# Second layer of a fused kernel: blocks 0 and 1 turned by another engine, rows' parts moved ahead of weight splits

## The chip, the cores and the metric

The kernel runs on one core of one Trainium2 chip. The metric is the device time of one execution in microseconds (us). Five engines work side by side, each with a queue of its own: TensorE (PE in the profile; PEld is its weight load), VectorE (DVE), ScalarE (ACT), GpSimd (POOL) and SyncE (SP), which here only issues DMAs.

## The reference, cut to what matters

Three layers are chained: causal attention with a decay, a mixture of experts that sends each of 2304 tokens to one of 8 experts, and a dense layer on all tokens.

```python
x = attn(q, k, v, f)                          # 2304 tokens x 512
e_idx = np.argmax(x @ w_gate + modality_bias[modality_id], axis=1)
for e in range(8):                            # first layer: 512 -> 1024 -> 512
    mask = e_idx == e
    h = np.maximum(x[mask] @ w1[e], 0.0)
    out[mask] = gate_w[mask, None] * (h @ w2[e])
h = out @ w_in                                # second layer: 512 -> 2048 -> 512
g = np.maximum(0.01 * h, h)
return (g @ w_out).astype(np.float32)
```

## The kernel before, in words

Every product of float32 operands is made from two parts: a high part (a rounded copy, made by ScalarE) and a low part (the difference, made by VectorE), so that each product costs three matmuls: high by high, high by low, low by high. Names end in h and l for the parts: xh, xl (an expert tile's turned rows), w1h, w1l and w2h, w2l (an expert's weights), hh, hl (the turned activations of an expert tile), fxh, fxl (the second layer's turned rows), gh, gl (its activations).

**First layer.** Tokens are sorted by expert into tiles of 128. There are at least 18 of them (NSTAT), and at most 25 (NS); the number is known at run time, and in this run it is 20, tiles 0 to 19. `step(t)` (L1165) does, for tile t, its first product (`gemm1`, 24 matmuls, into h), and for tile t-1 the turning of its activations (`trh`, L1114: 8 transposes into two PSUM tiles th, then hh by ScalarE and hl by VectorE) and its second product (`gemm2`, L1124: two halves of 12 matmuls into yp). Between these two halves `trx` (L207) turns the rows of tile t+1: 4 transposes into tx, then xh, xl. yp is a single PSUM bank. `yout` (L1129) empties it: ScalarE writes ys (a pool of two buffers, tag "ys"), GpSimd copies an index column into it and scatters the rows to yd in DRAM. For tiles from 17 on, `yout` comes at the beginning of a later step: `step(19)` begins with `yout(17)`. `split(t, 0, k)` and `split(t, 1, k)` make the parts of the first and the second weights where the expert changes, under a condition that ScalarE and VectorE read, and have SyncE load the next weights.

Inside a step all five engines keep the program's order, as it is written (`ordered(tc, MS2)`, all engines named). Steps 18 and later sit in nested conditions, and the last one leads to `tail` (L1142): here `tail(19)`, with `yout(18)`, `trh(19)`, both halves of `gemm2` for tile 19 and `yout(19)`.

**Second layer.** The rows in yd are taken in four blocks of 512 and one of 256. `xload(b)` (L994) fetches a block into xr, which has one buffer. Blocks 0 and 1 come as rows, four DMAs of 128 rows each; 16 transposes by TensorE turn a block (`xts`, L1013), and ScalarE and VectorE make fxh and fxl. Blocks 2 to 4 come in pieces of 128 elements such that VectorE alone can turn them (STREAM_TRANSPOSE, into a buffer xq), after which fxh and fxl are made from xq. Block 0 is turned in `tail`: three groups of four transposes ahead of the first half of `gemm2`, one between the halves. Block 1 is turned in the second layer's visits 2 and 3, one group of four transposes ahead of `g1` and one behind it in each. Their PSUM pool pfx has a single buffer.

`visit(v)` (L1407) does `g1` (12 matmuls into u, then us, gh, gl by ScalarE and VectorE in turn) for one piece of the hidden layer, and `g2` (12 matmuls into a) for the piece of the visit before. In visits 0 to 4 only TensorE's order is written out; a scheduler at build time orders the other engines by when it expects things to be ready, except that `keep_in_program_order` puts an instruction behind the one written before it on its engine.

Of the kernel before, what the change touches and what calls it, by code (L numbers as in the profile page):

```python
# [9 lines left out]
F32 = mybir.dt.float32  # L10
F32R = mybir.dt.float32r
BF16 = mybir.dt.bfloat16
I32 = mybir.dt.int32
# [6 lines left out]
P = 128  # L20
B, H, S, D = 4, 8, 576, 64
BH = B * H
DM = H * D
# [6 lines left out]
XW = DM + 1  # L30
NSTAT = NTOK // P
# [4 lines left out]
NKB, NFB, NGB = DM // P, FF // P, DFF // P  # L36
FT = 512
GS = 4
NFIX = NTOK % FT
FIX = NTOK - NFIX  # L40
# [4 lines left out]
SIDE = 2  # L45
SP = 2.0
TE = 3
TX = 3
PST = 3
MS = ['PE', 'Activation', 'DVE', 'Pool', 'SP']  # L50
MS2 = ['PE', 'Activation', 'DVE', 'Pool', 'SP']
# [25 lines left out]
def fused(ctx: ExitStack, tc, qk0, qk2, vp, f, mid, wg, mb, w1, w2, w_in, w_out, out):  # L77
    nc = tc.nc
# [7 lines left out]
    yd = dr.tile([NTOK, XW], F32, name="yd")  # L86
# [120 lines left out]
    def trx(t, pool, tag):  # L207
        ps = pool.tile([P, 512], F32, tag=tag, name=f"tx{t}")
        for k in range(NKB):
            nc.tensor.transpose(ps[:, k * P:(k + 1) * P], xg[t % 2][:, k * P:(k + 1) * P], ident)  # L210
        nc.scalar.copy(xh[t % 2], ps)
        nc.vector.tensor_sub(xl[t % 2], ps, xh[t % 2].bitcast(F32))
# [769 lines left out]
    t0 = 0  # L982
# [11 lines left out]
    def xload(b):  # L994
        t0, n = blocks[b]
        r = xp.tile([P, FT // P, XW], F32, tag="xr", name=f"xr{b}")
        if b > 1:
            XR[b] = r.rearrange("p c d -> p (c d)")[:, :4 * n]
            for j in range(4):
                nc.sync.dma_start(XR[b][32 * j:32 * j + 32].rearrange("b (q c) -> b q c", c=P), yd[t0:t0 + n, j * P:(j + 1) * P].rearrange("(q b) c -> b q c", b=32))  # L1000
            if t0 < FIX:
                nc.sync.dma_start(tid[:, t0 // P:(t0 + n) // P].unsqueeze(2), yd[t0:t0 + n, DM:].bitcast(I32).rearrange("(c p) o -> p c o", p=P))
            return
        for i in range(n // P):
            XR[b, i] = r[:, i]
            nc.sync.dma_start(XR[b, i], yd[t0 + i * P:t0 + (i + 1) * P, :])

    X = {}

# [3 lines left out]
    def xts(b, sb, psums, part=None):  # L1013
        t0, n = blocks[b]
        if b not in X:
            xtile(b, sb)
        xh, xl = X[b]
        for i in range(n // P) if part is None else part:
            c = slice(i * P, (i + 1) * P)
            if b > 1:  # L1020
                t = XQ[0].tile([P, 512], F32, tag="xq", name=f"xq{b}_{i}")
                tc.keep_in_program_order(nc.vector.transpose(t.rearrange("p (i k c) -> p i k c", i=4, k=NKB), XR[b][:, i * 512:(i + 1) * 512].rearrange("p (i c k) -> p i k c", i=4, k=NKB)))
                t = t.rearrange("p (i k c) -> p k i c", i=4, c=32)
                h, l = (x[:, :, c].rearrange("p k (i c) -> p k i c", c=32) for x in (xh, xl))
                tc.keep_in_program_order(nc.scalar.copy(h, t))
                tc.keep_in_program_order(nc.vector.tensor_sub(l, t, h.bitcast(F32)))
                continue
            r = XR[b, i]
            nc.gpsimd.tensor_copy(tid[:, t0 // P + i:t0 // P + i + 1], r[:, DM:].bitcast(I32))
            rk = r[:, :DM].rearrange("p (c k) -> p k c", k=NKB)  # L1030
            pool, tag = psums[i % len(psums)]
            ps = pool.tile([P, 512], F32, tag=tag, name=f"fx{b}_{i}")
            for k in range(NKB):
                nc.tensor.transpose(ps[:, k * P:(k + 1) * P], rk[:, k], ident)
            yield
            ps = ps.rearrange("p (k c) -> p k c", c=P)
            nc.scalar.copy(xh[:, :, c], ps)
            nc.vector.tensor_sub(xl[:, :, c], ps, xh[:, :, c].bitcast(F32))
            yield

    def xtr(*a):
        for _ in xts(*a):
            pass
# [47 lines left out]
    with tc.tile_pool(name="rt2", reuse_waits="tile", bufs=1) as rt2, \  # L1091
# [10 lines left out]
        w2l = [mw.tile([P, 2, DM], F32R, name=f"w2l{k}") for k in range(4)]  # L1102
        WL["2h"], WL["2l"] = w2h, w2l
        ysc = []
        hh = mw.tile([P, FF], F32R, name="hh")
        hl = mw.tile([P, FF], F32R, name="hl")
        gc = mw.tile([P, 2], F32, name="gc")
# [13 lines left out]
                nc.scalar.copy(hh[:, c], ps)  # L1121
                nc.vector.tensor_sub(hl[:, c], ps, hh[:, c].bitcast(F32))  # L1122

        def gemm2(t, k0, k1):  # L1124
            for k in range(k0, k1):
                for i, (ap, wp) in enumerate(((hh, w2h), (hh, w2l), (hl, w2h))):
                    nc.tensor.matmul(yp, lhsT=ap[:, k * P:(k + 1) * P], rhs=wp[k // 2][:, k % 2, :], start=(k == 0 and i == 0), stop=(k == NFB - 1 and i == 2))  # L1127

        def yout(t):  # L1129
            m, i = at_slot(oidx, t)  # L1130
# [11 lines left out]
        def tail(t):  # L1142
            with ordered(tc, MS4):
                if t >= LATE:
                    yout(t - 1)
                trh(t)
                ps = [(pmx, "tx"), (pma, "h"), (pmb, "h"), (pm0, "th")]
                xs_ = [xts(0, xp0, [p], [i]) for i, p in enumerate(ps)]
                for x in xs_[:3]:
                    next(x)  # L1150
                next(xs_[0])
                if t >= NSTAT:
                    split(t, 1, 3, True)
                gemm2(t, 0, 4)
                next(xs_[3])
                for x in xs_[1:]:
                    next(x)
                gemm2(t, 4, NFB)
                yout(t)

# [4 lines left out]
        def step(t):  # L1165
            nx = t + 1 < NS
            if t > LATE:
                yout(t - 2)
            if not t:
                with tc.issue_after(st["late"].ins):  # L1170
                    split(t, 1, 0)
                    split(t, 1, 1)
            if t == K1 - 1:
                flags(1, N2)
            keepg(t)
            if t > LATE:
                split(t, 0, 3)
            if t + 2 < NS and t + 2 != K1:
                gather(t + 2)
            if t:  # L1180
                gemm1(t, 0, 2, (pma, pmb)[t % 2], "h")
            aside(t, "load")
            if 0 < t < TE:
                trh(t - 1)
            if nx:
                split(t + 1, 0, 0)
            aside(t, "a1")
            aside(t, "a2")
            if t >= TE:
                trh(t - 1)  # L1190
            if t > NSTAT:
                split(t - 1, 1, 2)
            aside(t, "b")
            if nx:
                split(t + 1, 0, 1)
            aside(t, "pool")
            if t:
                gemm1(t, 2, 3, (pma, pmb)[t % 2], "h")
            if nx and t < NSTAT:
                split(t + 1, 0, 2)  # L1200
            if t:
                gemm1(t, 3, 4, (pma, pmb)[t % 2], "h")
                keep(t)
            if t > NSTAT:
                split(t - 1, 1, 3)
            if nx and t >= NSTAT:
                split(t + 1, 0, 2)
            if nx and 0 < t < LATE:
                split(t + 1, 0, 3)
            if t:  # L1210
                gemm2(t - 1, 0, 4)
            if nx and (0 < t < TX or t >= NSTAT - 1):
                trx(t + 1, pmx, "tx")
            if t:
                split(t, 1, 0)
                split(t, 1, 1)
            if nx and TX <= t < NSTAT - 1:
                trx(t + 1, pmx, "tx")
            if t == K1:
                next(fini, 0)  # L1220
            aside(t, "d")
            if t:
                gemm2(t - 1, 4, 8)
            if t < NSTAT:
                split(t, 1, 2)
            if 0 < t < LATE:
                yout(t - 1)
            if t < NSTAT:
                split(t, 1, 3)

        def finish():
            cnt, full, used = runb, early["full"], early["used"]
# [101 lines left out]
    with tc.tile_pool(name="fx", reuse_waits="tile", bufs=1) as fx, \  # L1334
# [5 lines left out]
         tc.tile_pool(name="pfu", reuse_waits="tile", bufs=3, space=PSUM) as pfu:  # L1340
        for i in range(GS, NSET):
            wset(fx, i)
        XQ.append(xq)
        G = {}
        A = {}
        Y = {}
# [60 lines left out]
        def visit(v):  # L1407
            b, fb = seq[v]
            parts = {}
            if fb < GS and b + 1 < NBK:  # L1410
                for k, i in (((2, 0), (2, 1), (3, 2), (3, 3)) if b == 0 else ((1, 0), (2, 1), (2, 2), (3, 3))):
                    if k == fb and i < blocks[b + 1][1] // P:
                        parts[i] = lambda b=b, i=i: xtr(b + 1, fx, [(pfx, "x")], [i])
            for i in sorted(parts)[:1 if v < GS else 2]:
                parts.pop(i)()
            g1(b, fb)
            for i in sorted(parts):
                parts.pop(i)()
            if v in XV:
                xload(XV[v])  # L1420
            if v:
                b, fb = seq[v - 1]
                g2(b, fb)
                if b == NBK - 1 and fb + NSET < NGB:
                    for i in range(2):
                        for _ in wpart(fb + NSET, i):
                            pass
                if v in WV:
                    for _ in wpart(*divmod(2 * GS + WV.index(v), 2)):
                        pass  # L1430
# [53 lines left out]
```

## Time and profile before

| | before |
|---|---|
| median of 3 runs | 857.75 us (857.01 to 859.49) |
| profiled execution, its own time | 857.52 us |
| span of that execution | 855.8 us |
| outside the span | 1.72 us |
| TensorE busy | 847.4 us, 99% of the span |
| TensorE's share of the chain that ended last | 94% |
| VectorE, ScalarE, GpSimd busy | 56%, 47%, 16% |
| granted TensorE clock | 1.0 of full speed in all 40 slices |

The span is the time from the first to the last instruction that the profiler saw. A busy TensorE is a queue of overlapping matmuls: a matmul of 128x512 is shown as 0.39 us long, and the next one starts 0.23 us after it. So the start of one instruction to the start of the next tells what it costs, and a larger distance is a stall even where no idle time is shown. The chain that ended last adds such distances up.

### The profile page before, as it was taken

Reading aid. Unit: us, or ns where it says so; the run is one execution under the profiler, and the core shown is the slowest. Engines: PE = TensorE matmul, PEld = TensorE weight load, DVE = VectorE, ACT = ScalarE, POOL = GpSimd, SP = SyncE. Lnnn points to the kernel's source line nnn. Section 1 sums busy time; section 2 is a strip of 40 time slices with the busy share of each in tenths; the row PEclk is TensorE's granted clock in tenths of the full one; section 3 lists DMA queues with packets and bytes.
Section 4 is the critical chain, followed back from the end, with each engine's and each line's share of the span. In section 5 each row is a group of like instructions: output and inputs, shape, how many; then the busy total and the mean of one; then the engine's idle time right before and its main releaser. Section 6 shows DMA issues by size and latency. Waiting matters only on the chain.

```text
span 855.8 us, 14440 instructions
## 1 busy us (share of the span) xinstructions
PE 847.4 (99%) x4724; PEld 700.8 (82%) x4724; DVE 479.0 (56%) x890; ACT 403.4 (47%) x857; POOL 133.2 (16%) x311
## 2 busy tenths in 40 slices
PE   8999999999999999999999999999999999999998
PEld 5888888888887888888888888888888888888887
DVE  7678777778757335233214456686338933473334
ACT  6888878877266355333323344553224422242222
POOL 5102222351146122112121000000000000001111
PEclk9999999999999999999999999999999999999999
DMA  6776787976385254132322231132002300011112
GB/s 210 194 188 178 204 214 201 235 206 207 94 295 190 64 173 137 59 96 75 100 53 66 51 74 50 54 119 75 0 1 74 102 22 1 1 50 50 49 50 74
DMA packets 36579, 92.72 MB, mean 108 GB/s; under 512 B 7017, under 2 KB 12809, under 8 KB 36490
## 3 DMA queue, kind: packets, MB, share of 16 engines
q1 hardware_dynamic: 31834, 76.95, 31.4%
q0 software_dynamic: 4640, 14.71, 5.5%
q8 instruction: 40, 0.66, 0.3%
q14 instruction: 49, 0.40, 0.1%
q10 hardware_dynamic: 16, 0.00, 0.0%
HBM read 131.63 MB, written 14.99 MB: 171 GB/s over the span
## 4 chain that ended last, share of the span: by engine, by line
PE 94%; DMA 2%; ACT 2%; DVE 1%; issue 0%; POOL 0%; SPq 0%; DVEq 0%
PE u L1358 23%; PE a L1378 23%; PE h L222 13%; PE yp L1127 13%; PE pv L547 5%; PE pt L535 3%; PE sc L446 2%; PE th L1119 2%; PE sc L447 2%; DMA aq<-aq 1%; PE xo L571 1%; PE tx L210 1%; ACT p L461 1%; PE pt L525 1%; PE sc L498 1%; PE sc L500 1%
## 5 line engine op out<-in xcount | busy, mean ns | idle before, releaser
L1360 ACT COPY us<-u 128x512 f32<-128x512 f32 (+1 forms) x80 | 43.4, 543 | 169.9 <-PE u L1358 169.5
L1361 DVE SCALAR_TENSOR_TENSOR us<-u,us 128x512 f32<-128x512 f32 (+1 forms) x80 | 50.9, 637 | 125.6 <-ACT us L1360 124.2
L1358 PE MATMUL u<-fxh,wloi 128*128 128x512 f32 (+1 forms) x320 | 117.2, 368 | 0.0
L1358 PE MATMUL u<-fxl,whii 128*128 128x512 f32 (+1 forms) x320 | 117.2, 368 | 0.0
L1358 PE MATMUL u<-fxh,whii 128*128 128x512 f32 (+1 forms) x320 | 116.3, 368 | 0.0
L1378 PE MATMUL a<-whio,gh 128*128 128x512 f32 x280 | 109.3, 391 | 0.0
L1378 PE MATMUL a<-wloo,gh 128*128 128x512 f32 x280 | 109.1, 390 | 0.0
L1378 PE MATMUL a<-whio,gl 128*128 128x512 f32 x280 | 101.9, 389 | 0.0
L461 ACT ACTIVATE p<-sc,nm 128x128 f32<-128x128 f32 (+3 forms) x128 | 66.1, 525 | 24.6 <-DVE nm L456 20.1
L1391 POOL DMA_INDIRECT out<-acc,tid x16 | 16.0, 1001 | 363.9 <-DVE acc L1385 343.7
L1358 PEld LDWEIGHTS u<-fxh,wloi 128*128 128x128 f32 x320 | 60.3, 188 | 10.5
L1358 PEld LDWEIGHTS u<-fxl,whii 128*128 128x128 f32 x320 | 60.3, 188 | 10.3
L1358 PEld LDWEIGHTS u<-fxh,whii 128*128 128x128 f32 x320 | 60.2, 188 | 10.3
L1363 ACT CAST gh<-us 128x512 fp32r<-128x512 f32 (+1 forms) x76 | 44.5, 586 | 49.1 <-DVE us L1361 39.0
L1364 DVE TENSOR_TENSOR gl<-us,gh 128x512 fp32r<-128x512 f32 (+1 forms) x76 | 49.2, 647 | 31.4 <-ACT gh L1363 29.9
L1122 DVE TENSOR_TENSOR hl<-th,hh 128x512 fp32r<-128x512 f32 x40 | 25.8, 686 | 71.9 <-ACT hh L1121 71.9
L456 DVE TENSOR_REDUCE nm<-sc 128x2 f32<-128x256 f32 (+1 forms) x64 | 51.1, 820 | 24.7 <-PE sc L452 18.7
L1127 PE MATMUL yp<-w2h,hh 128*128 128x512 f32 x160 | 64.5, 403 | 0.0
L1127 PE MATMUL yp<-w2h,hl 128*128 128x512 f32 x160 | 62.9, 393 | 0.0
L1127 PE MATMUL yp<-w2l,hh 128*128 128x512 f32 x160 | 62.5, 391 | 0.0
L1378 PEld LDWEIGHTS a<-whio,gl 128*128 128x128 f32 x280 | 52.5, 188 | 11.0
L1378 PEld LDWEIGHTS a<-whio,gh 128*128 128x128 f32 x280 | 52.6, 188 | 10.8 <-ACT gh L1363 0.4
(344 smaller groups left out, 1675.8 us busy)
## 6 DMA issues: line engine op xcount, KB each, us to landing
w1r<-w SPq DMA_DIRECT2D x86, 512.0 KB
w2r<-w SPq DMA_DIRECT2D x82, 512.0 KB
rwi<-w_in SPq DMA_DIRECT2D x16, 512.0 KB
rwo<-w_out SPq DMA_DIRECT2D x16, 512.0 KB
raw<-qk SPq DMA_DIRECT2D x14, 576.0 KB
vt<-vp SPq DMA_DIRECT2D x16, 320.0 KB
bk<-aq SPq DMA_DIRECT2D x14, 288.0 KB
bq<-raw SPq DMA_DIRECT2D x14, 288.0 KB
```

Of the source, the lines that this page charges most:

```text
L222: nc.tensor.matmul(Hp[t][:, n, :], lhsT=xp[t % 2][:, k * P:(k + 1) * P], rhs=wp[k][:, n * 512:(n + 1) * 512], start=(k == 0 and i == 0), s ...
L456: nc.vector.tensor_reduce(nm, view, axis=AX.X, op=ALU.max, negate=True)
L461: st["exp"] = nc.scalar.activation(pt[:, j, :], view[:, j, :], AF.Exp, bias=nm[:, j:j + 1], scale=1.0, accum_out=sms[g % 3][:, c, j:j + 1])
L547: nc.tensor.matmul(pv_[64 * j:64 * j + 64, q0:w], lhsT=vt[:, j, b, :], rhs=sb[:, j, b, q0:w], start=(b == 0), stop=(b == blocks[-1][0]))
L1122: nc.vector.tensor_sub(hl[:, c], ps, hh[:, c].bitcast(F32))
L1127: nc.tensor.matmul(yp, lhsT=ap[:, k * P:(k + 1) * P], rhs=wp[k // 2][:, k % 2, :], start=(k == 0 and i == 0), stop=(k == NFB - 1 and i == 2))
L1358: nc.tensor.matmul(ps, lhsT=w[:, k * P:(k + 1) * P], rhs=x[:, k, :], start=(i == 0), stop=(i == 3 * NKB - 1))
L1360: nc.scalar.copy(us, ps)
L1361: nc.vector.scalar_tensor_tensor(us, ps, 0.01, us, ALU.mult, ALU.max)
L1363: nc.scalar.copy(gh, us)
L1364: nc.vector.tensor_sub(gl, us, gh.bitcast(F32))
L1378: nc.tensor.matmul(A[b][i], lhsT=x[:, c], rhs=w, start=(first and m == 0), stop=(last and m == 2))
```

## The change

- `TX` goes. `trx(t + 1)` stands ahead of `split(t, 1, 0)` and `split(t, 1, 1)` in every step from 1 on; before, it stood behind them in steps 3 to 16.
- Block 0 is fetched in pieces, as blocks 2 to 4 are, with its token numbers by a DMA of its own instead of four copies on GpSimd. VectorE turns it. Its parts 0 and 1 stand in `step(18)` behind `trx(19)`, parts 2 and 3 at the end of `step(18)`. The 16 transposes in `tail` go. The buffers that VectorE turns into come from the "ys" pool.
- `gemm2`'s first half in `tail` puts its four low-part matmuls (hl) last.
- Block 1 is fetched half in pieces, half as rows. All four of its parts stand in visit 3 ahead of `g1`: parts 0 and 1 turned by VectorE, parts 2 and 3 by four transposes of TensorE each.

```diff
-TX = 3
@@ xload(b)
+        m = n // 2 if b == 1 else n
+        XR[b] = r.rearrange("p c d -> p (c d)")[:, :4 * m]
+        for j in range(4):
+            nc.sync.dma_start(XR[b][32 * j:32 * j + 32].rearrange("b (q c) -> b q c", c=P), yd[t0:t0 + m, j * P:(j + 1) * P].rearrange("(q b) c -> b q c", b=32))
+        for i in range(m // P, n // P):
             XR[b, i] = r[:, i]
             nc.sync.dma_start(XR[b, i], yd[t0 + i * P:t0 + (i + 1) * P, :])
+        if t0 < FIX:
+            nc.sync.dma_start(tid[:, t0 // P:(t0 + m) // P].unsqueeze(2), yd[t0:t0 + m, DM:].bitcast(I32).rearrange("(c p) o -> p c o", p=P))
@@ xts(b, sb, psums, part)
-            if b > 1:
-                t = XQ[0].tile([P, 512], F32, tag="xq", name=f"xq{b}_{i}")
-                tc.keep_in_program_order(nc.vector.transpose(...))
+            if (b, i) not in XR:
+                t = XQ[-1](b, i)
+                pin = tc.keep_in_program_order if b else (lambda x: x)
+                pin(nc.vector.transpose(...))
...
+                pin(nc.scalar.copy(h, t))
+                pin(nc.vector.tensor_sub(l, t, h.bitcast(F32)))
@@ first layer
+        XQ.append(lambda b, i: m2.tile([P, XW], F32, tag="ys", name=f"xq{b}_{i}")[:, :512])
@@ gemm2(t, k0, k1, late=False)
+            terms = [(k, i) for k in range(k0, k1) for i in range(3)]
+            if late:
+                terms = [x for x in terms if x[1] < 2] + [x for x in terms if x[1] == 2]
@@ tail(t)
-                ps = [(pmx, "tx"), (pma, "h"), (pmb, "h"), (pm0, "th")]
-                xs_ = [xts(0, xp0, [p], [i]) for i, p in enumerate(ps)]
-                for x in xs_[:3]:
-                    next(x)
-                next(xs_[0])
                 if t >= NSTAT:
                     split(t, 1, 3, True)
-                gemm2(t, 0, 4)
-                next(xs_[3])
-                for x in xs_[1:]:
-                    next(x)
+                gemm2(t, 0, 4, True)
+                if t < NSTAT:
+                    for i in range(4):
+                        xtr(0, xp0, None, [i])
                 gemm2(t, 4, NFB)
@@ step(t)
-            if nx and (0 < t < TX or t >= NSTAT - 1):
+            if nx and t:
                 trx(t + 1, pmx, "tx")
+            if t == NSTAT:
+                for i in range(2):
+                    xtr(0, xp0, None, [i])
             if t:
                 split(t, 1, 0)
                 split(t, 1, 1)
-            if nx and TX <= t < NSTAT - 1:
-                trx(t + 1, pmx, "tx")
...
             if t < NSTAT:
                 split(t, 1, 3)
+            if t == NSTAT:
+                for i in range(2, 4):
+                    xtr(0, xp0, None, [i])
@@ visit(v)
-                for k, i in (((2, 0), (2, 1), (3, 2), (3, 3)) if b == 0 else ((1, 0), (2, 1), (2, 2), (3, 3))):
+                for k, i in (((3, 0), (3, 1), (3, 2), (3, 3)) if b == 0 else ((1, 0), (2, 1), (2, 2), (3, 3))):
...
-            for i in sorted(parts)[:1 if v < GS else 2]:
+            for i in sorted(parts):
                 parts.pop(i)()
             g1(b, fb)
```

## Rows read from the trace of the kernel before

**Rows 1.** The page, part 1: busy us of each engine, share of span, instructions

```profile
PE 847.4 (99%) x4724; PEld 700.8 (82%) x4724; DVE 479.0 (56%) x890; ACT 403.4 (47%) x857; POOL 133.2 (16%) x311
```

**Rows 2.** Chain that ended last, steps 4 and 5: start us, us, engine tile line xcount

```profile
260.76 1.18 DVE w2l L177
261.95 0.61 DVE xl L212
262.60 2.13 PE h L222 x8
...
265.61 2.78 PE h L222 x12
```

**Rows 3.** Timeline of ScalarE, step 4: start us, us, instruction, count [idle before <-releaser]

```profile
257.63 2.00 ACT L173 CAST w2h<-w2r 128x1024 fp32r<-128x1024 f32 x2
```

**Rows 4.** Timeline of VectorE, step 4

```profile
257.24 2.42 DVE L177 TENSOR_TENSOR w1l<-w1r,w1h 128x1024 fp32r<-128x1024 f32 x2
```

**Rows 5.** Timeline of VectorE, step 18

```profile
433.22 0.69 DVE L212 TENSOR_TENSOR xl<-tx,xh 128x512 fp32r<-128x512 f32 x1 [5.10 <-ACTq L189]
```

**Rows 6.** Timeline of VectorE, second layer, block 2's parts 1 and 2

```profile
488.59 1.07 DVE L1022 STREAM_TRANSPOSE xq<-xr 128x512 f32<-128x512 f32 x1
490.35 0.69 DVE L1026 TENSOR_TENSOR fxl<-xq,fxh 128x512 fp32r<-128x512 f32 x1 [0.69 <-ACT fxh L1025]
490.96 1.08 DVE L1022 STREAM_TRANSPOSE xq<-xr 128x512 f32<-128x512 f32 x1
```

**Rows 7.** Timeline of ScalarE, step 19 and the tail

```profile
435.43 0.69 ACT L1133 ACTIVATE ys<-yp,gc 128x512 f32<-128x512 f32 x1 [2.24 <-PE yp L1127]
436.15 0.19 ACT L1112 COPY gc<-xg 128x1 f32<-128x1 f32 x1
449.06 1.06 ACT L1121 CAST hh<-th 128x512 fp32r<-128x512 f32 x2
```

**Rows 8.** Timeline of TensorE: step 19's second product, tail's first low-part matmul

```profile
441.62 0.39 PE L1127 MATMUL yp<-w2h,hh 128*128 128x512 f32 x1
441.85 0.39 PE L1127 MATMUL yp<-w2l,hh 128*128 128x512 f32 x1
444.38 0.60 PE L210 MATMUL tx<-ident,xg 128*128 128x128 f32 x4
450.49 0.50 PE L1127 MATMUL yp<-w2h,hl 128*128 128x512 f32 x1
```

**Rows 9.** Timeline of GpSimd: scatter of tile 16, block 1's last token numbers

```profile
428.78 1.03 POOL L1135 DMA_INDIRECT yd<-ys,oidx  x1 [14.05 <-DMA w1r<-w]
467.10 0.19 POOL L1029 COPY tid<-xr 128x1 int32<-128x1 int32 x1 [2.07 <-DMA xr<-yd]
```

**Rows 10.** Chain that ended last, the tail

```profile
448.61 1.45 PE fx L1034 x12
450.06 3.00 PE yp L1127 x12
453.06 0.47 PE fx L1034 x4
453.53 2.76 PE yp L1127 x12
```

**Rows 11.** Timelines of TensorE, ScalarE, VectorE, visit 2: one group of block 1's transposes

```profile
464.36 0.63 PE L1034 MATMUL fx<-ident,xr 128*128 128x128 f32 x4
464.75 0.48 PE L1358 MATMUL u<-fxh,whii 128*128 128x512 f32 x1
465.09 0.59 ACT L1037 CAST fxh<-fx 128x512 fp32r<-128x512 f32 x1 [1.31 <-PE fx L1034]
465.71 0.69 DVE L1038 TENSOR_TENSOR fxl<-fx,fxh 128x512 fp32r<-128x512 f32 x1 [1.21 <-ACT fxh L1037]
469.86 0.69 DVE L1364 TENSOR_TENSOR gl<-us,gh 128x512 fp32r<-128x512 f32 x1
```

**Rows 12.** Windows: us, busy us by engine (instructions), granted clock, DMA share, GB/s

```profile
260.00:264.00 4.00, 3.06 (x14) 2.19 (x13) 4.00 (x6) 2.77 (x5) 3.75 (x5) 1.00 0.49 157
```

## What the change should do

> **What bounds the kernel now.** I read the page's busy shares first. TensorE is busy 847.4 of 855.8 us, the other engines half of the time or less [rows 1]. So whatever takes TensorE work away or closes one of its gaps is worth its full length, and whatever makes TensorE wait costs its full length. Next comes the chain of work in order of time, because a stall of TensorE shows there as a piece that is longer than its twins. Last come the timelines around the places that the change touches, engine by engine, to see what each queue has in front of it. Three places matter: step 4, steps 18 and 19 with the tail, and the second layer's visits 2 and 3.
>
> **Rows' parts ahead of the splits (TX).** This edit acts in steps 3 to 16, but only where splits are really done and xl then comes late. The chain leaves TensorE once in that stretch: in step 5, where it runs over w2l and xl on VectorE before h goes on [rows 2]. From 260.76 to the end of that half of `gemm1` (262.60 + 2.13 = 264.73) are 3.97 us, while the twin half takes 2.78 [rows 2]: a stall of 1.2 us. The cause is the order on VectorE: w1l until 259.66 [rows 4], then two w2l, then xl at 261.95 [rows 2]. On ScalarE, xh stands behind two w2h of 2.00 us from 257.63 [rows 3]. With `trx` first, xh starts at about 258 and xl at 259.7, done by 260.4; it is wanted about 0.9 us after 260.76, so nothing is left of the stall. The w2h and w2l that now come 0.6 us later are wanted by the next `gemm2` of this tile, behind 264.73 plus another 2.78: covered by more than 4 us. In the other steps TensorE waits for no xl, so the edit gives nothing there. Sum: **-1.2 us** (bounds -1.2 and -0.9, if the first matmuls still meet a late piece).
>
> **Block 0 on VectorE, in step 18.** What this costs is decided by order, not by busy time. Each part is a chain of three: a turn on VectorE, the high part on ScalarE, the low part on VectorE. In block 2, from one turn to the next are 490.96 - 488.59 = 2.37 us, and from a turn to its low part 1.76 us [rows 6]. In a step all engines keep the written order, so nothing fills in or overtakes. Part 0 begins when xl of `trx(19)` ends, 433.22 + 0.69 = 433.9 [rows 5]. Part 3 turns at 433.9 + 3 x 2.37 = 441.0, and ScalarE is through with it at 442.8. Only then does its queue reach `yout(17)` (ys), which before ran at 435.43 [rows 7], and behind it gc and hh of tile 18. From ys to gc is 0.72 us, gc takes 0.19 [rows 7], so hh starts at 443.7 or later. The first half of `gemm2(18)` wants three things from there: yp emptied by that ys, hh, and hl. In the tail, where TensorE waits for the same pair, the first matmul with hl came 1.43 us after hh had started (449.06 to 450.49) [rows 7, 8]. That gives 445.1, and ten more matmuls at 0.23 (441.62 to 441.85) [rows 8] end the half at 447.4. Before, it ended at 444.38, where the next transposes start [rows 8]: 3.0 us later. Three conditions that ScalarE and VectorE now pass with a full queue lie in between; no row prices one on a path, nothing to 0.2 us each is my estimate, and I take 0.3 together. Sum: **+3.3 us** (bounds 2.5, if hh is reached sooner by some pipelining, and 4.0).
>
> Could it start later still? Part 1 turns into the ys buffer that the scatter of tile 16 reads. That scatter went out at 428.78 [rows 9], after the loads of block 0, which read the same DRAM tile. Pieces of 128 elements and the four-byte token numbers may take some us longer than rows did; part 1 turns at 436.3, so there are over 4 us of cover after the 1.03 us of the issue and its transfer. The four token copies that leave GpSimd, and the one more DMA in SyncE's queue, have no one waiting for them: price nothing, and if that cover were gone, the chain above would move by what is missing.
>
> **The tail.** The 16 transposes that go are twelve in 1.45 us and four in 0.47 us [rows 10]. The twelve stood while ScalarE made hh, started at 449.06 for the first of two [rows 7]; a single one of the pair is done near 449.65, and the transposes ended at 450.06 in the chain's count, of which the first matmul's own start-up is a part. So they covered a wait that stays: gain 0.1 at most, and I take none. The half after them took 3.00 us where its twin took 2.76 [rows 10], as its first hl came late; with the hl terms last that 0.24 goes. The four in between go whole: 0.47. Sum: **-0.8 us** (bounds -0.7 and -1.0).
>
> **Block 1 in visit 3.** Eight transposes go, two groups of 0.47 as in [rows 10]: -0.94. The two groups that stay now follow each other directly, and pfx has one buffer: the second group has to wait until ScalarE and VectorE have read the first. A group that starts at 464.36 lets its successor start at 464.75, while its low part ends at 465.71 + 0.69 = 466.40 [rows 11]: 2.04 - 0.39, with the release 1.7 us of stall. Before, groups were separated by 12 matmuls, which hid this. VectorE has gl of visit 2 done at about the time that visit 3 starts, then part 0's turn of 1.07 us [rows 6, 11], which fits into the 1.35 us before the low part is due. So 1.7 stands, and the sum is **+0.8 us** (bounds 0.6 and, if VectorE's parts 0 and 1 stand ahead of the low part, 3.8; nearest to the row in which nothing stands ahead, so I take 0.8). The rows' loads are in time: their last tile was there at 467.10 [rows 9], and the transposes that need it come some 3 us after that, now as before.
>
> **Sum.** -1.2 + 3.3 - 0.8 + 0.8 = +2.1 us. The profiled execution took 857.52 us, 855.8 of it span and 1.72 around it, which the change does not touch: 859.6. The median of the runs shown is 0.23 above that execution, so the forecast for a median is 857.75 + 2.1 = **859.8 us**, 0.24% slower.
>
> **The rivals.**
> *Step 18 hides the turning.* If ScalarE's queue were not held by parts 2 and 3 (if their copies are let behind ys and hh), the 3.3 goes: -1.2 - 0.8 + 0.8 = -1.2, 856.5 us. For it speaks that VectorE and ScalarE idle for most of that step (ScalarE waits 2.24 us ahead of ys [rows 7], VectorE 5.10 ahead of xl [rows 5]). Against it: in a step the order is as written.
> *Both waits vanish.* All 24 transposes and the late xl are gain: -1.2 - 0.8 - 0.94 = -2.9, 854.8 us. It needs a second buffer in pfx, or an order that I cannot see.
> *VectorE's parts go ahead in visit 3 (slower).* If the low part of the first group of transposes is queued behind turn and low part of both VectorE parts, it starts after 2 x 2.37 = 4.7 instead of 1.35 us: 3 us more, 862.9 us. It decides from the point where part 0's low part is put ahead of it. Against it: the build-time scheduler filled such gaps elsewhere.
> [...]
> [...]
> *The change does nothing.* If xl was late for another cause than order, and turning and waits cancel: within 1 us of 857.75; I count it to the forecast's lower side.
>
> **How the numbers follow.** Forecast 0.62 (its own range 858.3 to 861.3), step 18 hidden 0.14, both waits gone 0.06, VectorE's parts ahead 0.10, clock 0.08. The range has to leave out no more than 0.2: from 856.0 (the hidden case with half a us) to 862.7 (the clock case) it leaves out both waits gone and VectorE's parts ahead, 0.16, and the edges of the rest. About 0.3%, 2.6 us, is what a measurement of this kernel can tell from no change: 855.2 to 860.3. Faster by more: 0.07 (both waits gone, and a little). Slower by more: the two slow cases 0.18 and about a quarter of the forecast, 0.15: 0.33. Within: 0.60.
>
> **What would show it.** Right: step 5 with two equal halves of h; in step 19 the first half of `gemm2` starting some 3 us late behind ys and hh, with ScalarE's four copies of block 0 in a row before them; in the tail hh directly ahead of yp and an even row of 12 matmuls; in visit 3 a gap of some 1.7 us between two groups of four transposes. Wrong: ys of tile 17 within 1 us of the end of its product, a granted clock below 1.00 after the wait, or the two groups back to back. Most of all the forecast hangs on the 2.37 us from part to part: at 1.4 us step 18 would hide the work.

## The result and the profile after

| | before | after |
|---|---|---|
| median of 6 runs, side by side on one chip | 857.31 us (856.29 to 859.49) | 863.28 us (862.78 to 865.20) |
| ratio after / before, 95% interval | | 1.0071 (1.0057 to 1.0085) |
| profiled execution, its own time | 857.52 us | 863.1 us |
| its span | 855.8 us | 861.2 us |
| its mean granted TensorE clock | 1.0 | 0.995 |

The change costs 863.28 - 857.31 = 6.0 us, 0.7%. The forecast was +2.1 us; the result lies 0.6 us above the upper end of the range.

The page of the kernel after, its lines on busy time and on TensorE's granted clock, which answer to [rows 1]:

```profile
PE 847.3 (98%) x4700; PEld 700.2 (81%) x4700; DVE 486.1 (56%) x896; ACT 404.0 (47%) x857; POOL 134.9 (16%) x305
PEclk9999999999999999999989999999999999999999
```

24 transposes are gone (4724 to 4700 matmuls), yet TensorE's busy time is the same to 0.1 us. Something has made the remaining ones longer. One slice of the 40 shows a lower granted clock: the 21st, 431 to 452 us, which holds steps 18 and 19.

To say where the time went, the span is cut at the starts of the same instructions in both traces: the first `th` transposes of the first layer (tile 0), those of tiles 4, 18 and 19, and the first matmul into u, which opens the second layer. What lies ahead of the first cut (the attention) is untouched by the change, and its length differs from one execution to the next, by up to 7.45 us in the traces of this case. So all distances below start at the first cut.

| stretch | before, us | after, us | difference | forecast |
|---|---|---|---|---|
| first th to th of tile 4 (the TX edit) | 52.19 | 50.98 | -1.21 | -1.2 |
| to th of tile 18 | 173.40 | 173.43 | 0.0 | 0 |
| to th of tile 19 (step 19, behind block 0's turning) | 9.60 | 17.35 | **+7.75** | +3.3 |
| to first u (the tail) | 8.55 | 7.77 | -0.78 | -0.8 |
| to the end (second layer, visit 3) | 399.68 | 400.41 | +0.73 | +0.8 |
| sum | 643.42 | 649.94 | +6.5 | +2.1 |

The two traces differ by 6.5 us and the medians by 6.0, as a trace is one execution. Four of the five stretches came as forecast. One stretch, 9.6 us long before, holds the whole miss. The chain of work that ended last in the kernel after, step 19 to visit 3 (start us, us, what):

```profile
441.62 5.49 PE h L221 x12
447.11 2.88 PE yp L1130 x12
...
455.17 5.79 PE yp L1130 x24
...
474.60 0.49 PE fx L1033 x4
...
475.73 0.70 DVE fxl L1037
...
476.48 0.75 PE fx L1033 x4
```

The second half of `gemm1(19)` takes 5.49 us; its twin in step 5 takes 2.78 [rows 2]. The tail's second product is one even row of 24 (5.79 us), in place of the transposes, 3.00 and 2.76 of [rows 10]. In visit 3 the chain leaves TensorE between two groups of four transposes. TensorE's waits in 425 to 480 us (engine, line, waited for; us in total, times, longest), where the kernel before shows none at all:

```profile
PE h L221 <- ACTq L188: 4.9, 1, 4.9
PE fx L1033 <- DVE fxl L1037: 1.4, 1, 1.4
PE yp L1130 <- ACT hh L1121: 1.1, 1, 1.1
```

So TensorE did not wait for ys or hh of tile 18 first, as forecast. It waited one product earlier, in `gemm1(19)`, for ScalarE's queue at L188: that is the `If` in `split`. The timeline of TensorE in step 19:

```profile
435.67 1.04 PE L1119 MATMUL th<-ident,hs 128*128 128x128 f32 x8
441.62 1.22 PE L221 MATMUL h<-w1h,xh 128*128 128x512 f32 x2 [4.92 <-ACTq L188]
442.64 1.05 PE L221 MATMUL h<-w1l,xh 128*128 128x512 f32 x2
...
446.91 0.55 PE L1130 MATMUL yp<-w2h,hh 128*128 128x512 f32 x1
447.30 0.39 PE L1130 MATMUL yp<-w2l,hh 128*128 128x512 f32 x1
```

and that of ScalarE in steps 18 and 19, to be held against [rows 7]:

```profile
432.64 0.62 ACT L1024 CAST fxh<-xq 128x512 fp32r<-128x512 f32 x1 [1.75 <-DVE xq L1021]
435.03 0.62 ACT L1024 CAST fxh<-xq 128x512 fp32r<-128x512 f32 x1 [1.77 <-DVE xq L1021]
437.64 0.62 ACT L1024 CAST fxh<-xq 128x512 fp32r<-128x512 f32 x1 [1.99 <-DVE xq L1021]
440.00 0.62 ACT L1024 CAST fxh<-xq 128x512 fp32r<-128x512 f32 x1 [1.75 <-DVE xq L1021]
440.53 0.68 ACT L1136 ACTIVATE ys<-yp,gc 128x512 f32<-128x512 f32 x1
441.24 0.19 ACT L1112 COPY gc<-xg 128x1 f32<-128x1 f32 x1
441.64 1.07 ACT L1121 CAST hh<-th 128x512 fp32r<-128x512 f32 x2 [0.20 <-ACTq L188]
```

Four copies of block 0 stand in a row, 2.4 to 2.6 us apart, each idle until VectorE has turned its part. Behind them come ys, gc, the condition and hh. TensorE starts at 441.62, in the moment in which ScalarE is past the condition. In the built program the queue of ScalarE, and below it that of TensorE, read as follows (`waits Activation` is a wait for a semaphore that ScalarE counts):

```
837 L1024 CAST fxh0_6138<-xq0_3_6308 128x4x128 [waits DVE_49]
...
839 L1136 ACTIVATE ys17_6319<-yp_3252,gc_3251 128x512 [waits PE_49,DMASW2_49,Activation_49,Pool_49]
840 L1112 COPY gc_3251<-xg1_108 128x1 [waits DMASW3_49,Activation_49]
...
842 L188 COMPARE_AND_BRANCH
843 L172 CAST w1h2_111<-w1r2_101 128x1024 [waits DMAHW5_49]
844 L172 CAST w1h3_112<-w1r3_102 128x1024 [waits DMAHW6_49]
...
847 L1121 CAST hh_3249<-th18_0_6357 128x512 [waits PE_49]

2118 L1119 MATMUL th18_1_6364<-ident_63,hs_2669 128x128 x3
2119 L188 UNCONDITIONAL_BRANCH
2120 L221 MATMUL h19_6344<-w1h2_111,xh1_2670 128x512 [waits Activation_49]
```

The condition is `split(19, 0, 3)`: it would make new first weights w1h[2], w1h[3] if the expert changed at tile 19. Here it doesn't, and nothing is written (no CAST at L172 stands in the timeline). But only ScalarE and VectorE read the condition. In the built program TensorE has no other sign that nothing is coming, so the matmul that reads w1h[2] waits until ScalarE is past it. (VectorE passes the same condition, behind its last part of block 0, which ended at 441.34; ScalarE was the later of the two, and no run moves one without the other.)

Then the clock. Windows of the kernel after (us, busy us of PE, PEld, DVE, ACT, POOL with instructions, granted clock, DMA share, GB/s):

```profile
437.00:440.00 3.00, 0.00 (x0) 0.00 (x0) 2.29 (x3) 0.62 (x1) 0.18 (x1) 1.00 0.00 0
440.00:441.00 1.00, 0.00 (x0) 0.00 (x0) 0.35 (x1) 1.00 (x2) 0.00 (x0) 0.71 0.00 0
441.00:442.00 1.00, 0.38 (x1) 0.38 (x2) 0.35 (x1) 0.76 (x3) 0.00 (x1) 0.50 0.00 0
442.00:446.00 4.00, 4.00 (x10) 3.09 (x10) 1.29 (x2) 0.71 (x2) 2.26 (x3) 0.50 0.47 92
...
447.00:448.00 1.00, 1.00 (x6) 0.81 (x5) 0.00 (x0) 0.85 (x1) 0.00 (x0) 0.88 0.31 78
```

While TensorE is idle the granted clock goes from 1.00 to 0.50, and comes back after 447, when TensorE has worked for some 5.5 us. All of the half product runs at 0.50: pairs of matmuls start 0.85 us apart (442.64, 443.50), against 0.46 before.

The 7.75 us of this stretch then come out by starts. The kernel before shows there:

```profile
437.97 1.04 PE L1119 MATMUL th<-ident,hs 128*128 128x128 f32 x8
438.76 0.71 PE L222 MATMUL h<-w1h,xh 128*128 128x512 f32 x2
...
447.57 1.03 PE L1119 MATMUL th<-ident,hs 128*128 128x128 f32 x8
```

After the change, from th to that half of h are 441.62 - 435.67 = 5.95 us, before 438.76 - 437.97 = 0.79: +5.16, of which 4.92 are idle. The half takes 446.91 - 441.62 = 5.29 us, before, at a clock of 1.00, 441.62 [rows 8] - 438.76 = 2.86: +2.4. The first matmul of yp takes 0.39 to its successor instead of 0.23: +0.2.

### The profile page after: what moved, and what is told of

It reads as the page before. It is cut to its first block, busy times and chain, and to the rows that moved or that the text cites. A ratio compares the mean times of both kernels' runs of the same rounds, so it can differ in the third digit from the quotient of the medians.

```text
span 861.2 us, 14391 instructions
## 1 busy us (share of the span) xinstructions
PE 847.3 (98%) x4700; PEld 700.2 (81%) x4700; DVE 486.1 (56%) x896; ACT 404.0 (47%) x857; POOL 134.9 (16%) x305
```

## The experiments

Theory A (the condition): TensorE waits for the condition ahead of hh, each part of block 0 that ScalarE's queue has in front of it costs one period of 2.4 us, and the clock adds its own. Rival B: ys and hh hold it, as in the prediction's step. Rival C: something else in the change, such as new DMAs or the buffers of ys. For each run a median, and the ratio to the kernel before on the same chip with its 95% interval, are given; "first th to end" is the distance from the table above (643.4 before, 649.9 after).

**e1_rows_first: the TX edit alone.** Kernel before with

```diff
-            if nx and (0 < t < TX or t >= NSTAT - 1):
+            if nx and t:
                 trx(t + 1, pmx, "tx")
...
-            if nx and TX <= t < NSTAT - 1:
-                trx(t + 1, pmx, "tx")
```

> The kernel before with only the order of the rows' parts changed: trx ahead of the second weights' splits in steps 3 to 16 too. Theory: the late xl of step 5 goes (3.97 us of a half that should take 2.78), and nothing else moves: 1.2 us faster than before, ratio 0.9986, and the half in step 5 takes 2.8 us. Rival: the splits that come 0.6 us later are wanted soon after, and the stall only moves: no change, 0.0 us.

Measured: 857.85 us, ratio 0.9980 (0.9966 to 0.9993). First th to end 642.43: -1.0 us. First th to th of tile 4 is 50.98, -1.21, as in the kernel after. This edit is a gain by itself, and step 5's wait was one of order.

**e2_block0_as_before: the change without block 0.** Kernel after with block 0 fetched as rows and turned in `tail` by TensorE, as before (`xload`, `tail` and the two places in `step` put back).

> The changed kernel with block 0 as it was: fetched as rows, turned by TensorE in the tail, nothing of it in step 18, the terms of the tail's second product in the old order. Rows' parts first and block 1 half and half stay. Theory (all the loss lies in step 19, where TensorE waits for what stands behind block 0's parts in ScalarE's queue): the 7.6 us of step 19 go, the 0.8 us of the tail come back, 863.3 - 7.6 + 0.8 = 856.5, that is 0.8 us faster than before give or take 0.5. Rival (the loss comes from loads in pieces or from block 1's order in visit 3): 860 or more.

Measured: 858.99 us, ratio 0.9992 (0.9977 to 1.0006). From th of tile 18 to th of tile 19 are 9.60 us, as before, and TensorE has no wait there; the wait of 1.4 us in visit 3 is as in the kernel after (first u to end 400.63). First th to end is 643.25, only 0.2 us less than before where 0.8 were expected: -1.2 for the TX edit, +0.95 in the second layer. So the 7.75 us belong to block 0's turning, not to block 1's DMAs, and rival C is left only as far as it comes with block 0.

**e3_condition_first: only the condition moved.** It goes ahead of block 0's parts 2 and 3:

```diff
-            if t > LATE:
+            if t > LATE and t != NSTAT + 1:
                 split(t, 0, 3)
...
             if t == NSTAT:
+                split(t + 1, 0, 3)
                 for i in range(2, 4):
                     xtr(0, xp0, None, [i])
```

> The changed kernel with one thing moved: the condition under which the first weights' pieces 2 and 3 of tile 19 are split stands ahead of block 0's parts 2 and 3 (end of step 18) and not behind them (begin of step 19). Theory (TensorE's 4.9 us of idle time are the wait for ScalarE to pass that condition, because the second half of gemm1 reads the weights that it may write): the second half of gemm1 follows the transposes at once; then the first half of gemm2 for tile 18 waits some 3.1 us for ys and hh, as the prediction had it. If the clock stays at 1.00 over that shorter wait: 863.3 - 7.6 + 3.1 = 858.8; if it falls, some 2 us more. Rival (TensorE waits for ys, or for VectorE's parts themselves, and not for the condition): the second half of gemm1 still begins some 5 us late, 863.

Measured: 863.09 us, ratio 1.0033 (1.0014 to 1.0053). The timeline of TensorE in step 19 of this kernel:

```profile
438.87 1.04 PE L1119 MATMUL th<-ident,hs 128*128 128x128 f32 x8
439.67 0.71 PE L221 MATMUL h<-w1h,xh 128*128 128x512 f32 x2
...
445.49 0.50 PE L1130 MATMUL yp<-w2h,hh 128*128 128x512 f32 x1 [2.80 <-ACT hh L1121]
```

With the same instructions on every engine and one condition earlier, the half of h follows th at once: theory A. And now the wait that the prediction named appears where it had been put, at `gemm2(18)` behind ys and hh, with 2.80 us. The chain that ended last runs there over block 0's parts 2 and 3, ys, gc and hh to yp, as the prediction had it, with no DMA on it. So rival B was the second in line, and of rival C nothing shows in this stretch. The stretch takes 14.54 us against 17.35; it is not nearer to 9.60 because the clock fell here too (windows, columns as above):

```profile
446.00:447.00 1.00, 1.00 (x4) 0.70 (x4) 0.76 (x2) 0.96 (x1) 0.69 (x2) 0.94 0.08 16
447.00:448.00 1.00, 1.00 (x4) 0.71 (x4) 0.00 (x0) 0.07 (x1) 0.99 (x2) 0.50 0.68 246
```

This half of yp took 4.82 us in the chain, against 2.76 [rows 10]: 2.1 us for the clock.

**e4_filler: the wait kept, its idle time filled.** 21 matmuls of bf16 into an unused tile stand between `trh(18)` and the second half of `gemm1(19)`; they only keep TensorE at work, and their result is not used.

```diff
                 trh(t - 1)
+            if t == NSTAT + 1:
+                fill = pmx.tile([P, 512], F32, tag="tx", name="fill")
+                for _ in range(21):
+                    nc.tensor.matmul(fill, lhsT=onesb, rhs=onesb..., start=True, stop=True)
```

> The changed kernel with 21 matmuls of constants (128x512, bf16, result unused) on TensorE between the transposes of tile 18's activations and the second half of gemm1 for tile 19, about as long as the wait there (21 x 0.23 = 4.8 us). Theory (the clock falls because TensorE idles; the half that follows then takes 5.3 instead of 2.8 us): granted clock 1.00 throughout, the half takes 2.8 us, and the kernel is 2.4 us faster than the changed one: 860.9. Rival (that half is slow because its weights or its rows come late): no change, 863.

Measured: 864.16 us, ratio 1.0045 (1.0032 to 1.0059), by ratios 2.2 us less than the kernel after. Timeline and windows of TensorE:

```profile
441.26 4.70 PE L1192 MATMUL fill<-onesb 128*128 128x512 bf16 x21
446.39 0.74 PE L221 MATMUL h<-w1h,xh 128*128 128x512 f32 x2 [0.43 <-ACTq L188]
```

```profile
441.00:446.00 5.00, 4.96 (x25) 2.22 (x23) 3.47 (x5) 1.82 (x3) 0.18 (x1) 1.00 0.01 3
446.00:450.00 4.00, 3.61 (x16) 2.95 (x17) 1.40 (x3) 1.79 (x4) 2.27 (x3) 1.00 0.25 74
```

The half of h starts as late behind th as in the kernel after (446.39 - 440.39 = 6.00, there 5.95), still released by the condition, but the granted clock stays 1.00, and the half takes 3.05 us in the chain instead of 5.49. First th to end is 647.5: 2.4 us less. That is the clock's part, taken away by itself.

**e9_three_parts: one part less ahead of the condition.** Only part 3 moves, from the end of step 18 to behind hs(19). (The lines left out at the head of this diff and of e5's serve the case of 19 tiles, which this run doesn't take.)

```diff
...
+            if t == NSTAT + 1:
+                xtr(0, xp0, None, [3])
...
-                for i in range(2, 4):
+                for i in range(2, 3):
                     xtr(0, xp0, None, [i])
```

> The changed kernel with block 0's part 3 alone moved, behind hs of tile 19: three parts instead of four stand ahead of the condition. Theory (the wait is what is left of a chain of parts of 2.4 us each): TensorE's idle time ahead of the second half of gemm1 falls from 4.9 to 2.5 us. What the clock does is open: if it stays at 1.00, the half takes 2.8 us and the kernel is 4.8 us faster than the changed one, 858.5; if it falls as it did after 2.8 us in e3_condition_first, 2.4 us faster, 860.9. Rival (a fixed cost of the conditions, not the parts): 4.9 us stay.

Measured: 863.49 us, ratio 1.0047 (1.0031 to 1.0064). TensorE's wait and the windows:

```profile
443.93 0.73 PE L221 MATMUL h<-w1h,xh 128*128 128x512 f32 x2 [2.55 <-ACTq L188]
```

```profile
444.00:445.00 1.00, 1.00 (x5) 0.83 (x6) 0.44 (x1) 1.00 (x2) 0.69 (x1) 1.00 0.00 0
445.00:446.00 1.00, 1.00 (x4) 0.79 (x3) 0.85 (x2) 0.02 (x1) 0.69 (x2) 0.55 0.23 66
```

4.92 - 2.55 = 2.37 us for one part, the period of [rows 6] to the digit. The clock fell in this execution too, about 1 us after TensorE had resumed; the half took 4.52 us, 1.7 more than at full clock. So the wait was about halved, and 13.99 - 9.60 = 4.4 of the stretch's 7.75 us stayed.

**e5_parts_later: two parts out of the way.** Part 2 goes behind hh and hl of tile 18, part 3 behind hs(19), both in step 19.

```diff
...
             if t > NSTAT:
                 split(t - 1, 1, 2)
+            if t == NSTAT + 1:
+                xtr(0, xp0, None, [2])
...
+            if t == NSTAT + 1:
+                xtr(0, xp0, None, [3])
...
-            if t == NSTAT:
-                for i in range(2, 4):
-                    xtr(0, xp0, None, [i])
```

> The changed kernel with block 0's parts 2 and 3 moved from the end of step 18 into step 19: part 2 behind hh and hl of tile 18, part 3 behind hs of tile 19. Nothing else differs. Theory (what hurts is only what stands behind the parts in ScalarE's and VectorE's queues: the condition for the first weights, ys and hh): all 7.6 us of step 19 go, the clock stays at 1.00, and of the change remain -1.2 (rows' parts first), -0.8 (tail) and +0.7 (visit 3): 1.3 us faster than before, ratio 0.9985. Rival (four parts do not fit into two steps beside the rest; hs or the tail's hh are held instead): a wait of 1 us or more in step 19 or in the tail, 859 or more.

Measured: 859.43 us, ratio 0.9999 (0.9983 to 1.0015). The wait at the condition is 0.4 us, and th to th takes 10.23 us: moving two parts takes 17.35 - 10.23 = 7.1 of the 7.75 us away, clock included. But first th to end is 643.48, 1.4 us more than expected, in two places: 0.63 in this stretch, of which 0.61 lie between th and that half of h (1.40 us from start to start, 0.79 before), 0.37 of them idle; and 0.66 in the tail (8.43 us to first u, against 7.77 after). There the chain of this kernel reads:

```profile
452.00 0.04 ACTq L1324
...
454.80 0.04 ACTq L1136
...
454.97 0.10 ACT ys L1136
```

Between a branch of ScalarE (L1324, from step 19 into the tail) and its next instruction lie 2.75 us, which the trace puts down to nothing that it shows. ys then starts 1.62 us after th of tile 19 (453.35), and hh behind it. In the kernel before, xh ends at 445.60 and ys starts at 448.47, 0.90 after th: a pause of like length, but most of it lies beside the end of the product. Here part 3's copy has made xh 0.5 us later against th, and the branch, at 452.00 behind xh's end at 451.89, passes that on. My expectation had left this out.

**e6_groups_apart and e7_two_banks: the wait in visit 3.** Both are e5 with one more edit. e6 puts one group of block 1's transposes into visit 2 again (`(2, 2), (3, 0), (3, 1), (3, 3)`) and its two DMAs of rows first; e7 gives the second group a PSUM bank of another pool (`[(pfx, "x"), (pfu, "u")]`).

> The kernel of e5_parts_later, and block 1's two groups of transposes apart: part 2 ahead of g1 in visit 2, part 3 ahead of g1 in visit 3, and the two DMAs of rows ahead of the pieces in xload(1). Theory (1.4 us of idle time between the groups are the wait for the one buffer of pfx): no idle time there, 1.65 us faster than e5_parts_later, 2.9 us faster than before, ratio 0.9966. Rival (the rows are not there by visit 2, or VectorE's parts now come late for g1 of block 1): no gain over e5_parts_later.

> The kernel of e5_parts_later, with both groups of block 1's transposes in visit 3 as there, but the second group written into a buffer of pfu (three buffers) instead of pfx's one. Theory (the buffer, and nothing else, holds the second group): the groups follow each other within 0.4 us, 1.65 us faster than e5_parts_later, as e6_groups_apart. Rival (VectorE's or ScalarE's order there holds TensorE, whatever the bank): the 1.4 us of idle time stay, or move ahead of g1 of block 1.

Measured: e6 857.39 us, ratio 0.9986 (0.9971 to 1.0001); e7 857.86 us, ratio 0.9988 (0.9973 to 1.0002). First u to end: 398.83 and 398.78 us, against 400.42 in e5: -1.6 us each. The chain of e7 shows the two groups as one:

```profile
470.75 0.95 PE fx L1033 x8
471.70 2.77 PE u L1361 x12
```

Two different ways round the single buffer give the same 1.6 us, so the buffer was the cause. Against the kernel before, first th to end is 1.8 us shorter in e6 (641.61) and 1.85 in e7 (641.57), not 2.9, as e5 had fallen short.

**e8_spread: all repairs together.** e6, and part 0 of block 0 goes into step 18's `gemm1` (behind hs(18)), part 1 behind `trx(19)`, so that each part has a place of its own in which ScalarE idled.

> The kernel of e6_groups_apart with block 0's part 0 moved up in step 18, from behind trx(19) to behind hs of tile 18, so that one part stands in each of four gaps of the two steps. In the trace of e6_groups_apart two parts behind trx(19) still held the condition for 0.4 us (TensorE's idle time ahead of the second half of gemm1 in step 19), and part 3 pushed ScalarE's way into the tail, so that hh of the last tile came 0.4 us later than before. Theory (both are the parts' places in the queues): both go, 0.8 us faster than e6_groups_apart, measured from the first transposes of the experts' layer to the end 640.8 us against 641.6 there and 643.4 before. Rival (part 0 waits for block 0's load and now holds xh of tile 19): no gain or a stall in step 19's first half of gemm1.

Measured: 857.45 us, ratio 0.9976 (0.9965 to 0.9988): 2.1 us, 0.24%, faster than the kernel before, and it beats both kernels. First th to end is 640.78, -2.6 us. TensorE's waits in 425 to 482 us:

```profile
PE yp L1130 <- ACT hh L1121: 1.2, 1, 1.2
```

Only the tail's wait is left. Against e1 (0.9980) the medians tell no difference; by distances it is 1.65 us shorter.

## Why the prediction was wrong

**What held.** The TX edit: step 5 now has two even halves of h, 2.79 and 2.87 us from start to start, where the first had 0.94 us of wait in it; -1.21 us for -1.2, and e1 shows it alone. The timeline of TensorE after, to be held against [rows 2]:

```profile
259.45 0.63 PE L221 MATMUL h<-w1h,xh 128*128 128x512 f32 x2
...
262.24 1.03 PE L1119 MATMUL th<-ident,hs 128*128 128x128 f32 x8
263.03 0.71 PE L221 MATMUL h<-w1h,xh 128*128 128x512 f32 x2
...
265.90 0.40 PE L1130 MATMUL yp<-w2h,hh 128*128 128x512 f32 x1
```

The tail: -0.78 for -0.8, hh directly ahead of an even row of yp. Visit 3: the groups start 2.04 us apart in TensorE's timeline (474.44 and 476.48), as worked out from [rows 11], and cost +0.73 for +0.8; e6 and e7 confirm the single buffer. The rival in which VectorE's parts go ahead in visit 3 didn't come: the low part of the first group came at 475.73, directly behind its high part. (Its price was off: 4.7 - 1.35 is 3.4 us, not 3.)

**ScalarE's queue held too.** Step 18 came 2.30 us earlier in this trace (th of tile 18 at 435.67, before 437.97). The prediction had ys at 442.8 and hh at 443.7 or later: less 2.3 that is 440.5 and 441.4. Measured: 440.53 and 441.64. The period from part to part was 2.36 to 2.61 us, and the three conditions took about as much as had been taken for them: 0.3 us was an estimate that no row priced, measured were 0.25 for the two between parts 1 and 2 (a period of 2.61 instead of 2.36 us) and 0.20 for the one ahead of hh. Part 1 turned at 433.90, directly behind part 0, so its ys buffer was free in time. (`yout(16)`, whose scatter frees it, stands at the beginning of `step(18)`: tile 16 is already among those whose `yout` comes in a later step.)

**The step that failed** is the sentence "The first half of `gemm2(18)` wants three things from there: yp emptied by that ys, hh, and hl." It asked when ScalarE gets to hh, rightly, but not who wants something from ScalarE before that. The conditions stood in the sum as time that ScalarE needs to pass them, and not as something for which TensorE waits. The second half of `gemm1(19)` wants the condition behind gc, and it wants it one half product, 2.85 us, sooner than `gemm2(18)` wants hh. With the prediction's own times: ScalarE past gc at 443.7 or so, TensorE there 0.80 us after th, at 437.97 + 0.80 = 438.8: 4.9 us of wait instead of 3.0. e3, with the condition moved, shows the other wait by itself: 2.80 us at hh.

**The clock** had a chance of 0.08 and a price of 2.8 us; it came, with 2.4 us (e4), and it came on top of the wait. No run shows the 2.8: it was an estimate, the 2.76 us of a half product [rows 10] taken twice. What the runs showed in its place are 2.4 us (e4), 2.1 (e3) and 1.7 (e9). The low chance rested on [rows 12], which only said that the clock read 1.00 around 0.94 us of idle time. With a forecast wait of 3 us, longer than any of TensorE's in the trace (1.1 us at most), there was no row for "it stays", and none for a fall. The trace of the kernel after has one: 1.00 to 0.50 within the idle 4.92 us, and back at 0.88 in 447 to 448. Where no row spoke for either, 0.08 was too little. By both corrections the sum would have been -1.2 + 4.9 + 2.4 - 0.8 + 0.8 = +6.1; the runs' medians gave +6.0.

**The range** ended at the clock case of the wrong wait, so the time lay outside it. Neither error alone would have done it: the longer wait alone gives 857.75 - 1.2 + 4.9 - 0.8 + 0.8 = 861.5, the clock alone 859.8 + 2.8 = 862.6. The range had no case in which both come. Nor did the clock need the longer wait: it fell in e3 too, whose wait of 2.80 us is about the one forecast, and cost 2.1 us there. So its chance was too low even for the forecast's own wait.

**What stays open** is what decides whether the clock falls. In e3 and e9 it doesn't in every execution. One fall as in their traces takes 1.7 of some 862 us, 0.002 of the mean granted clock. Two of the ten timed executions of e3 and one of the four of e9 (862.62 us) have a mean of 1.000, which leaves no room for such a fall; the others have 0.992 to 0.998, in which the attention can have had a share. All six of the kernel after have 0.995 to 0.997.

## What to carry to other kernels

When work is put into an in-order queue, list everything behind it that another engine waits for, conditions that are not taken among it, and find the consumer that comes first; the time at which the queue gets to the obvious result is not the answer. In the kernel after, a condition under which nothing was written held the matmul that reads what it might have written for 4.92 us, until ScalarE was past it; with the condition ahead of two of the parts (e3) that matmul started 0.80 us after th. So put such conditions ahead of slow chains, or spread the slow chain over the places in which the queue idles (e8). Price a new TensorE wait of some us also with the half product at 0.50 of the clock behind it, as a case of its own in the sum: where the clock fell in step 19, waits of 2.55 to 4.92 us cost 1.7 to 2.4 us more.

## What the runs showed of the hardware

- **The clock can fall after the wait is over, and the length of the wait alone does not settle it.** With 4.92 us idle it fell during the wait. With 2.80 us (e3) and 2.55 us (e9) it was still 1.00 when TensorE resumed, and 0.50 some 1 to 1.5 us later, for 3 us and more. With 1.1 us (tail) and 1.4 us (visit 3), both in the kernel after, it stayed at 1.00; with 1.80 us (e5's tail) the 24 matmuls behind the wait took 5.76 us, against 5.79 in the kernel after. So an idle time next to which the clock reads 1.00 is not yet one that costs nothing: look at the stretch behind it. But in the attention of the same traces, where TensorE waits for a load, it stayed at 1.00 after 2.26 us in e2 and fell after 2.20 us in e8 (TensorE's timeline and windows, columns as above, first e2, then e8):

```profile
173.20 0.30 PE L445 MATMUL sc<-ak,aq 128*128 128x128 f32 x1 [2.26 <-DMA aq<-aq]
173.00:178.00 5.00, 4.80 (x38) 4.14 (x40) 3.02 (x4) 2.81 (x12) 4.09 (x15) 1.00 0.18 45
172.27 0.30 PE L445 MATMUL sc<-ak,aq 128*128 128x128 f32 x1 [2.20 <-DMA aq<-aq]
173.00:176.00 3.00, 3.00 (x16) 2.91 (x16) 1.47 (x3) 0.59 (x1) 2.36 (x10) 0.50 0.10 31
```

- **Between a branch of ScalarE into the tail and its next instruction lie 2.42 to 2.75 us:** 2.75 in e5, 2.62 in e6, and in e8, from the branch at 446.58 to the next instruction at 449.05, 2.42 between the two. The conditions at L188 behind them show 0.04 us each in the same chains. What takes the time isn't shown.
